# A routing, a mixture of experts and an MLP on one core: low parts of the last weights taken a step later in the first routing, and more idle products

## The chip, the cores and the metric

The kernel runs on one core of a Trainium2 chip. The metric is the device time in microseconds (us) of one execution: the median of three runs is 817.9 us (817.57 to 819.57). Engines are named as in the profile: PE (TensorE, with its weight loads PEld), DVE (VectorE), ACT (ScalarE), POOL (GpSimd) and SP (SyncE, which here only issues transfers).

## The reference, cut to what matters

```python
# 1 attention with a state per head: (4, 8, 768, 40) -> rows x of 3072 tokens, 320 wide
# 2 experts: every token goes to one of 8 experts, 384 tokens each
logits = x @ w_gate
order = np.argsort(-logits.flatten())
for idx in order:                       # best (token, expert) pairs first
    tok, e = int(idx) // E, int(idx) % E
    if assigned[tok] >= 0 or counts[e] >= cap: continue
    assigned[tok] = e; counts[e] += 1
for e in range(E):
    mask = assigned == e
    out[mask] = np.maximum(x[mask] @ w1[e], 0.0) @ w2[e]
# 3 a common MLP on all tokens
h = out @ w_in                          # 320 -> 2048
g = np.where(h > 0, h, np.exp(np.minimum(h, 0)) - 1)
return g @ w_out                        # 2048 -> 320
```

Here `w_in` and `w_out` come as 64-bit floats. The kernel fetches their words and puts 32-bit floats together from them on the chip.

## The kernel before, in words

Attention runs first, until about 167 us, 24 units of work in a fixed order. The routing then finds, in eight rounds, one expert each, which expert fills up next and which 384 tokens it takes. Round 0 has nothing else to hide behind: the products of expert 0 need its tokens. So round 0 is written out by hand in `Mlp.start` (L1340), and the seven later rounds are woven into the products.

A round is a search: in each of six steps DVE compares 24 values per partition with 32 candidates (`ge`, L713), PE counts (L727), DVE folds the counts (L590 to L596), PE sums them (L748), and DVE picks the digit (L751, L754). Step 0 uses a comparison that was made during attention (L737). At the end DVE marks the tokens (L773 to L777), writes which weights to fetch (`wi`, L765), PE numbers the tokens (L783 to L785), and after twelve more products (L810) DVE writes the list of tokens, `idx` (L816).

Between these steps `start` calls a generator, `fill` = `wout_pieces` (L942), ten times. It prepares the last weights, `w_out`, in 16 chunks of 128 x 320. Chunk i goes through these pieces: SP fetches its words (L856, two chunks ahead); ACT takes the absolute value and, in one of two variants, the sign (L868, L870) and DVE shifts (L873); DVE puts the bits together (L880) and POOL multiplies by the sign (L883); ACT or DVE copies the rounded high part to `woh` (L972 or L974); POOL subtracts it to leave the low part `wol` (L965). In the other variant DVE adds the sign (L877) instead of ACT and POOL. Each `yield` ends a piece and says which engine the next one needs. One call of `start` runs pieces until a piece whose need names DVE ("d") is followed by a piece whose need names DVE too:

```python
while True:
    d = "d" in need
    _, need = next(fill)
    if d and "d" in need:
        break
```

What is left of the 16 chunks when round 0 ends is done among the products of expert 0, piece by piece, by a planner (`Mlp.run`). The planner counts expected engine times, runs a piece of `wout` first of all side work where its time has come, and holds it back where DVE's expected backlog is over 2 us. It pauses side work from the last product of the first MLP layer (`C0` = 7) until the first output product. The output product of chunk f (`C2`, L1234, L1235, L1238) needs both `woh` and `wol` of chunk f.

When `idx` is known, POOL issues three gathers of token rows (`xg`, L984 by `get_x`) behind three gathers of expert weights (`stg`). PE transposes each row tile when it has landed (L1049), ACT and DVE split it into two parts (L1066, L1057), and then the products of expert 0 start (L1096). Between these, PE runs idle products (`spin`, L1035) whose results nobody reads: `WARM` = [8, 2, 2, 2] says how many stand ahead of each transposed tile and behind the last. Engines run their own queue in order, so an idle product delays what stands behind it.

Of the kernel before, what the change touches and what calls it, by code (L numbers as in the profile page):

```python
# [8 lines left out]
F32 = mybir.dt.float32  # L9
# [4 lines left out]
ALU = mybir.AluOpType  # L14
# [14 lines left out]
FU = 3  # L29
SPIN, MX = 12, [256, 512, 640]  # L30
NB, NL, PX = 2, 3, 0.2
WARM = [8, 2, 2, 2]


class Plan:
# [46 lines left out]
    def next(self):  # L82
        self.due(min(self.todo)[0])
# [741 lines left out]
class Mlp:  # L825
# [115 lines left out]
    def wout_pieces(self):  # L941

        nc = self.nc
        wide = self.wout.dtype != F32
        n = 320
        tiles = {}

        def get(i):
            x = self.pool.tile([128, n, 2], I32, name="wx", bufs=3) if wide else None
            t = self.pool.tile([128, 2, n], F32, name="wt", bufs=2)  # L950
            tiles[i] = (x, t[:, 1], t[:, 0])
            self.fetch([(slice(0, 128), self.src(self.wout, slice(0, 128), slice(i * n, i * n + n)))], wide, tiles[i])

        get(0)
        get(1)
        yield
        for i in range(16):
            if i < 14:
                get(i + 2)
            F = tiles[i][2]  # L960
            yield self.plan.t, "d"
            yield from self.conv(wide, tiles.pop(i), not self.router.res or self.plan.pick(p=821 + PD, d=402) == "p")
            t = self.copy(self.woh[:, i], F, 360, 240)
            yield t, "p"
            nc.gpsimd.tensor_tensor(self.wol[:, i], F, self.woh[:, i], op=ALU.subtract)  # L965
            self.plan.on("p", 821)
            self.wdone = i + 1

    def copy(self, out, x, a, d):

# [69 lines left out]
    def prep_x(self, r):  # L1040
# [6 lines left out]
        def turn(k):  # L1047
            for t in range(3):
                nc.tensor.transpose(ps[k][0][:, t * 128:t * 128 + 128], self.xg[k][:, t * 128:t * 128 + 128], self.ident)  # L1049

        def split(k):
            p, slot = ps[k]
            p = p.rearrange("p (t n) -> p t n", t=3)
            h, l = (x[:, :, k * 128:k * 128 + 128] for x in (xh, xl))

            def rest():
                nc.vector.tensor_tensor(l, p, h, op=ALU.subtract)  # L1057
                slot[0] = plan.on("d", 469)
                if k == 2:
                    self.xst[r] = (xh, xl)  # L1060
                    self.xready[r] = slot[0]

            if r:
                plan.later(self.copy(h, p, 371, 469), rest)
            else:
                nc.scalar.activation(h, p, AF.Copy)  # L1066
                plan.on("a", 371)
                rest()

        if r == 0:  # L1070
            ps = [self.psum() for t in range(3)]
            for k in range(3):
                self.spin(WARM[k])
                turn(k)
                split(k)
            self.spin(WARM[3])
            return
# [262 lines left out]
    def start(self, first):  # L1340

        nc = self.nc
        fill = self.fill
        self.ws = {}
        early = []
        need = "d"
        for k, (_, _, gap) in enumerate(first):
            if gap and k > FK:
# [3 lines that stand above are left out]
                    if d and "d" in need:  # L1352
                        break
            if not early and 0 in self.router.res:
                for i in range(3):
                    self.get_w(0, i)
                early = [q for i in range(3) for q in self.pieces(i)]
        self.routed = 0
        self.get_x(0)
        for h, l, x, p in early:  # L1360
            nc.scalar.activation(h, x, AF.Copy)
        for k, (h, l, x, p) in enumerate(early):
            nc.vector.tensor_tensor(l[p], x[p], h[p], op=ALU.subtract)
            if k % 2 and k < 4:
                self.get_w(0, 3 + k // 2)
        self.wsplit = 3
        routes = self.routes(1)
        for _ in range(R1):
            next(routes)
        plan = self.plan  # L1370
        plan.reset()
        self.junk = self.acc.tile([128, 512], F32, name="acc")
        for _ in self.prep_x(0):
            pass
        return fill, routes
# [134 lines left out]
```

## Time and profile before

| | value |
|---|---|
| median of three runs | 817.9 us |
| profiled execution, its own time | 817.59 us |
| its span, first to last instruction | 815.8 us |
| mean granted clock of PE | 0.925 of 2.4 GHz |
| busy: PE, DVE, ACT, POOL | 89%, 72%, 43%, 38% |

The profile gives for each instruction its start and its length, and for idle time before it what ended that idle time. "Granted clock" is the share of 2.4 GHz that PE was given; it has two levels, 0.5 (1.2 GHz) and 1.0 (2.4 GHz), and a value between them is a mean over a stretch in which it changed. A line such as L972 can be that of a helper that several callers use.

### The profile page before, as it was taken

How to read it: one execution, taken by the hardware profiler on the slowest of the kernel's cores; microseconds unless marked ns; L12 is line 12 of the kernel's file. 1: busy time of each engine (PE TensorE's matmuls, PEld its weight loads, DVE VectorE, ACT ScalarE, POOL GpSimd, SP SyncE). 2: the span in 40 equal slices, each digit the busy share in tenths (PEclk: the TensorE clock that was granted, in tenths of full speed). 3: DMA queues.
4: the chain of work that ended last, by engine and by line, in shares of the span. 5: the costliest groups of instructions: out<-in, count | busy, mean ns of one | idle time of the engine just before them, and what ended most of it. 6: DMA issues, size and time to landing. Idle time of an engine off the chain costs nothing.

```text
span 815.8 us, 18330 instructions
## 1 busy us (share of the span) xinstructions
PE 729.8 (89%) x7355; PEld 681.9 (84%) x7355; DVE 586.1 (72%) x1616; ACT 348.5 (43%) x743; POOL 309.2 (38%) x358
## 2 busy tenths in 40 slices
PE   7788788836899799799999999999999999999995
PEld 5678678725788789789989988898999999999995
DVE  8697878777979976987897679867733942862542
ACT  5343334324356533543553255325533633742431
POOL 3687887626425631633134125213410601201001
PEclk8678787856999999999999999999999999999998
DMA  8766855135114202112123103200500410100000
GB/s 343 253 216 209 278 186 187 43 107 199 54 30 139 83 27 78 51 44 100 32 65 93 40 0 106 67 27 0 172 12 13 138 35 25 65 1 26 1 1 25
DMA packets 20757, 72.79 MB, mean 89 GB/s; under 512 B 3200, under 2 KB 7296, under 8 KB 19264
## 3 DMA queue, kind: packets, MB, share of 16 engines
q1 hardware_dynamic: 8336, 35.08, 12.6%
q0 software_dynamic: 8448, 31.73, 11.8%
q10 hardware_dynamic: 3888, 4.82, 2.1%
q8 instruction: 58, 0.95, 0.5%
q14 instruction: 27, 0.22, 0.1%
HBM read 62.96 MB, written 8.65 MB: 88 GB/s over the span
## 4 chain that ended last, share of the span: by engine, by line
PE 58%; DVE 21%; issue 8%; ACT 4%; DMA 4%; POOL 2%; ACTq 1%; SPq 0%; POOLq 0%; DVEq 0%
PE ph L1096 24%; PE acc L1234 5%; PE acc L1238 4%; PE acc L1235 4%; PE acc L1203 3%; PE acc L1205 3%; PE acc L1204 3%; DVE e L1149 2%; DMA xd<-x 2%; PE pr L727 2%; DVE ge L713 1%; DVE gl L980 1%; PE acc L1190 1%; PE pX L448 1%; DMA vk<-in_vk_dram 1%
## 5 line engine op out<-in xcount | busy, mean ns | idle before, releaser
L1234 PE MATMUL acc<-woh,gh 128*128 128x320 f32 x384 | 122.7, 320 | 0.0
L1238 PE MATMUL acc<-woh,gl 128*128 128x320 f32 x384 | 119.7, 312 | 0.0
L1235 PE MATMUL acc<-wol,gh 128*128 128x320 f32 x384 | 119.0, 310 | 0.0
L1149 DVE SCALAR_TENSOR_TENSOR e<-e,ph 128x384 f32<-128x384 f32 x128 | 69.9, 549 | 61.8 <-ACT e L1146 61.4
L1145 ACT ACTIVATE e<-ph 128x384 f32<-128x384 f32 x128 | 62.7, 489 | 116.3 <-PE ph L1096 112.0
L980 POOL TENSOR_TENSOR gl<-e,gh 128x384 fp32r<-128x384 f32 x33 | 34.8, 1057 | 164.3 <-DVE gh L974 132.3
L1096 PE MATMUL ph<-yh,wih 128*128 128x384 f32 x256 | 89.7, 351 | 0.4
L1096 PE MATMUL ph<-yh,wil 128*128 128x384 f32 x256 | 86.2, 337 | 0.0
L1113 ACT ACTIVATE gh<-ph 128x384 fp32r<-128x384 f32 x64 | 31.3, 491 | 121.9 <-PE ph L1096 120.7
L1244 POOL DMA_INDIRECT out_dram<-ot,idx x24 | 24.0, 1001 | 141.3 <-ACT ot L972 138.1
L1120 DVE SCALAR_TENSOR_TENSOR gl<-ph,gh 128x384 fp32r<-128x384 f32 x64 | 35.4, 556 | 56.8 <-ACT gh L1113 56.4
L1238 PEld LDWEIGHTS acc<-woh,gl 128*128 128x128 f32 x384 | 72.5, 189 | 0.6
L1234 PEld LDWEIGHTS acc<-woh,gh 128*128 128x128 f32 x384 | 72.8, 190 | 0.2
L1235 PEld LDWEIGHTS acc<-wol,gh 128*128 128x128 f32 x384 | 72.7, 189 | 0.0
L1146 ACT ACTIVATE e<-e 128x384 f32<-128x384 f32 x128 | 67.3, 526 | 4.0
L1096 PE MATMUL ph<-yl,wih 128*128 128x384 f32 x256 | 66.5, 341 | 0.0
L980 DVE TENSOR_TENSOR gl<-e,gh 128x384 fp32r<-128x384 f32 x95 | 57.3, 607 | 1.9
L1096 PEld LDWEIGHTS ph<-yh,wih 128*128 128x128 f32 x256 | 48.4, 189 | 4.5 <-ACT yh L1208 4.4
L1096 PEld LDWEIGHTS ph<-yh,wil 128*128 128x128 f32 x256 | 48.3, 189 | 0.0
L1096 PEld LDWEIGHTS ph<-yl,wih 128*128 128x128 f32 x256 | 46.4, 189 | 0.0
L1096 PE MATMUL ph<-xh,w1h 128*128 128x384 f32 x128 | 45.0, 352 | 0.2
L1203 PE MATMUL acc<-gh,w 128*128 128x384 f32 x128 | 44.6, 349 | 0.0
(269 smaller groups left out, 2023.5 us busy)
## 6 DMA issues: line engine op xcount, KB each, us to landing
vk<-in_vk_dram SPq DMA_DIRECT2D x12, 968.0 KB, 8.7
qk<-in_qk_dram SPq DMA_DIRECT2D x11, 1024.0 KB, 8.0
wx<-in_wout_dram SPq DMA_DIRECT2D x16, 320.0 KB, 2.8
xd<-x ACTq DMA_DIRECT2D x48, 96.0 KB, 3.7
cx<-in_win_dram SPq DMA_DIRECT2D x8, 512.0 KB, 4.4
qk<-in_qk_dram SPq DMA_DIRECT2D x2, 512.0 KB, 5.9
cx<-in_win_dram SPq DMA_DIRECT2D x4, 256.0 KB, 4.2
xg<-xd,idx POOLq DMA_INDIRECT x24, 3.3
```

The source lines that it names most:

```text
L980: (self.nc.vector if e == "d" else self.nc.gpsimd).tensor_tensor(out, x, y, op=ALU.subtract)
L1096: PE.matmul(p, w, x, start=k == 0, stop=k == 7)
L1113: nc.scalar.activation(h, p, AF.Relu)
L1120: nc.vector.scalar_tensor_tensor(l, p, 0.0, h, op0=ALU.max, op1=ALU.subtract)
L1145: nc.scalar.activation(e, p, AF.Relu, scale=-1.0)
L1146: nc.scalar.activation(e, e, AF.Exp, scale=-1.0)
L1149: nc.vector.scalar_tensor_tensor(e, e, -1.0, p, op0=ALU.add, op1=ALU.max)
L1203: PE.matmul(p, w[:, c], h, start=f == 0, stop=False)
L1204: PE.matmul(p, w[:, cl], h, start=False, stop=False)
L1234: PE.matmul(p, h[:, c], self.woh[:, f], start=f == 0, stop=False)
L1235: PE.matmul(p, h[:, c], self.wol[:, f], start=False, stop=False)
L1238: PE.matmul(p, l[:, c], self.woh[:, f], start=False, stop=f == 15)
```

## The change: a piece of the fill moves, and idle products are added

Four things change. First, in round 0 the low part of a chunk is no longer subtracted right behind its copy; it is kept in `late` and issued in front of the next chunk's copy (`self.routed < 0` holds only in round 0). The copy then no longer ends with `yield t, "p"`. Second, the tile `wt` (two halves, two buffers) becomes two tiles: `wa` with the pool's two buffers and `wt` with three. Third, `WARM` grows from [8, 2, 2, 2] to [20, 3, 3, 3]. Fourth, six idle products are issued as soon as `wi` of round 0 is written, and the accumulator they write is taken earlier for that. The buffers of the output rows, `ot`, stay three.

```diff
-WARM = [8, 2, 2, 2]
+WARM = [20, 3, 3, 3]
...
-            t = self.pool.tile([128, 2, n], F32, name="wt", bufs=2)
-            tiles[i] = (x, t[:, 1], t[:, 0])
+            tiles[i] = (x, self.pool.tile([128, n], F32, name="wa"), self.pool.tile([128, n], F32, name="wt", bufs=3))
...
+        def low(i, F):
+            nc.gpsimd.tensor_tensor(self.wol[:, i], F, self.woh[:, i], op=ALU.subtract)
+            self.plan.on("p", 821)
+            self.wdone = i + 1
+
+        late = None
...
             yield from self.conv(wide, tiles.pop(i), not self.router.res or self.plan.pick(p=821 + PD, d=402) == "p")
+            if late:
+                late = low(*late)
             t = self.copy(self.woh[:, i], F, 360, 240)
+            if self.routed < 0:
+                late = i, F
+                continue
             yield t, "p"
-            nc.gpsimd.tensor_tensor(self.wol[:, i], F, self.woh[:, i], op=ALU.subtract)
-            self.plan.on("p", 821)
-            self.wdone = i + 1
+            low(i, F)
...
+        self.junk = self.acc.tile([128, 512], F32, name="acc")
         self.ws = {}
...
             if not early and 0 in self.router.res:
+                self.spin(6)
                 for i in range(3):
...
         plan.reset()
-        self.junk = self.acc.tile([128, 512], F32, name="acc")
         for _ in self.prep_x(0):
```

## Rows read from the trace of the kernel before

**Rows 1.** Busy time by stretch: start and end, length, then busy us (and instructions) of PE, PEld, DVE, ACT and POOL, then PE's granted clock, the transfers' share and GB/s. The stretches are the search of round 0, the arrival of the tokens, and five stretches of the products.

```profile
166.00:186.50 20.50, 4.89 (x63) 3.80 (x63) 17.70 (x80) 6.52 (x15) 6.98 (x8) 0.50 0.36 106
192.00:200.00 8.00, 6.15 (x21) 4.11 (x19) 5.30 (x11) 4.29 (x9) 5.26 (x5) 0.56 0.69 235
200.00:216.00 16.00, 12.72 (x74) 11.80 (x75) 15.06 (x41) 7.51 (x17) 8.39 (x9) 1.00 0.28 92
216.00:238.00 22.00, 21.14 (x126) 18.66 (x125) 15.88 (x58) 9.25 (x19) 4.15 (x5) 0.92 0.15 45
238.00:278.00 40.00, 32.85 (x217) 30.70 (x216) 38.62 (x104) 23.50 (x50) 23.78 (x24) 0.99 0.28 88
278.00:295.00 17.00, 16.93 (x106) 15.56 (x107) 16.27 (x52) 10.13 (x23) 8.70 (x10) 0.91 0.24 79
295.00:816.00 521.00, 499.27 (x3152) 474.95 (x3151) 339.94 (x978) 220.56 (x449) 132.18 (x144) 0.99 0.15 49
```

**Rows 2.** The timeline of DVE in the search: start, length, line, operation. The comparisons of steps 1, 3 and 5 (of five; step 2's is as long as step 1's, step 4's as step 5's), and two of the instructions that mark the tokens.

```profile
169.43 0.56 DVE L713 TENSOR_TENSOR ge<-d,kx 128x768 bf16<-128x768 bf16 x1
...
175.31 1.11 DVE L713 TENSOR_TENSOR ge<-d,kx 128x768 bf16<-128x768 bf16 x1
...
182.05 1.10 DVE L713 TENSOR_TENSOR ge<-d,kx 128x768 bf16<-128x768 bf16 x1
185.48 0.65 DVE L773 SCALAR_TENSOR_TENSOR AB<-d,j,a 128x24 f32<-128x24 f32 x1
186.05 0.23 DVE L774 SCALAR_TENSOR_TENSOR AB<-d,j,a 128x24 f32<-128x24 f32 x1
```

**Rows 3.** The timeline of POOL in the same stretch, with idle time before an instruction and its releaser in brackets, and the first gather of token rows.

```profile
175.12 0.88 POOL L965 TENSOR_TENSOR wol<-wt,woh 128x320 fp32r<-128x320 f32 x1 [0.58 <-ACT woh L972]
177.05 0.87 POOL L883 TENSOR_TENSOR wt<-wt,wx 128x320 f32<-128x320 f32 x1 [1.04 <-issue]
...
185.22 0.87 POOL L965 TENSOR_TENSOR wol<-wt,woh 128x320 fp32r<-128x320 f32 x1 [0.58 <-ACT woh L972]
192.18 0.95 POOL L984 DMA_INDIRECT xg<-xd,idx  x1 [1.42 <-DVE inc L820]
194.73 1.21 POOL L984 DMA_INDIRECT xg<-xd,idx  x1 [0.30 <-issue]
```

**Rows 4.** The timeline of DVE in steps 2 and 3: pieces of the fill and the search's instructions behind them.

```profile
174.49 0.31 DVE L873 TENSOR_SCALAR wt<-wx 128x320 int32<-128x320 int32 x1
176.43 0.48 DVE L880 SCALAR_TENSOR_TENSOR wt<-wt 128x320 int32<-128x320 int32 x1
176.98 0.17 DVE L590 SCALAR_TENSOR_TENSOR fold<-pr,rem 32x8 f32<-32x8 f32 x1
178.21 0.17 DVE L751 TENSOR_REDUCE j<-pr 128x1 f32<-128x8 f32 x1
```

**Rows 5.** The timeline of PE from the numbering of the tokens to the first product of expert 0. A row with x8 is eight instructions, from the first start to the last end.

```profile
186.62 0.20 PE L783 MATMUL pr<-mm,ones 128*128 128x48 bf16 x1 [1.72 <-DVE mm L777]
189.44 0.99 PE L810 MATMUL pr<-R,ge 128*128 128x48 bf16 x12 [2.55 <-DVE R L803]
190.24 3.76 PE L1038 MATMUL acc<-wih 128*128 128x512 f32 x8
195.74 0.90 PE L1049 MATMUL ph<-ident,xg 128*128 128x128 f32 x3 [1.74 <-DMA xg<-xd,idx]
196.29 1.20 PE L1038 MATMUL acc<-wih 128*128 128x512 f32 x2
198.79 0.61 PE L1049 MATMUL ph<-ident,xg 128*128 128x128 f32 x3
...
199.98 0.44 PE L1096 MATMUL ph<-xh,w1h 128*128 128x384 f32 x1
```

**Rows 6.** The chain of work that ended last, around the first gather: start, length, what.

```profile
192.18 3.52 DMA xg<-xd,idx
...
199.43 0.50 ACT xh L1066
```

**Rows 7.** Busy time by stretch again (columns as in rows 1), two stretches of 2 us: before and at the rise of the clock.

```profile
192.00:194.00 2.00, 2.00 (x5) 0.99 (x3) 1.57 (x4) 0.75 (x3) 1.52 (x2) 0.50 0.83 318
198.00:200.00 2.00, 1.89 (x9) 1.15 (x8) 0.60 (x2) 0.98 (x2) 0.66 (x1) 0.74 0.83 264
```

**Rows 8.** What PE and its weight loads waited for from 200 to 300 us: us in total, times, the longest.

```profile
PEld ph L1049 <- DVE e L1149: 5.0, 1, 5.0
...
PE pr L727 <- DVE ge L713: 4.0, 2, 3.2
```

**Rows 9.** The timeline of POOL and PE among the products of expert 0: the low parts of chunks 9, 14 and 15, and the first output product of chunk 15.

```profile
244.90 0.88 POOL L965 TENSOR_TENSOR wol<-wt,woh 128x320 fp32r<-128x320 f32 x1 [2.70 <-DVE woh L974]
276.88 0.86 POOL L965 TENSOR_TENSOR wol<-wt,woh 128x320 fp32r<-128x320 f32 x1
286.52 0.87 POOL L965 TENSOR_TENSOR wol<-wt,woh 128x320 fp32r<-128x320 f32 x1
293.70 0.30 PE L1234 MATMUL acc<-woh,gh 128*128 128x320 f32 x1
```

**Rows 10.** DVE and POOL in one timeline at 205 us: three POOL subtractions back to back, and a DVE instruction of 8 values per partition that starts beside the first of them.

```profile
205.51 3.45 POOL L980 TENSOR_TENSOR w<-stg,w 128x512 fp32r<-128x512 f32 x3
205.70 1.26 DVE L690 SCALAR_TENSOR_TENSOR rem<-neg,rem 128x8 f32<-128x8 f32 x1
```

## Prediction

> **What bounds the kernel now.** I read the busy time by stretch first [rows 1]. From 295 us PE is busy 499 of 521 us at a granted clock of 0.99: the change touches nothing there. The change acts where PE isn't the bound. In the search of round 0 DVE is busy 17.7 of 20.5 us and PE 4.9; then the tokens' arrival takes until 200 us. After that come two stretches in which DVE is nearly full (15.1 of 16 us, and 38.6 of 40 us) while PE loses 3.3 and 7.2 us. So the end moves with the first product of expert 0, at 199.98 [rows 5], and with what DVE-bound work stands behind it.
>
> The timeline of DVE comes second [rows 2]. The same comparison takes 0.56 us in steps 1 and 2 and 1.10 in steps 3 to 5. POOL's timeline [rows 3] shows why: a low part L965 begins 0.19 us before each long one and runs 0.88 us. The comparison of 175.31 ends at 176.42, 0.42 after POOL's end at 176.00, so it waits for POOL's whole instruction and then runs in about 0.45. In the same way L773 takes 0.65 beside the L965 of 185.22, where its neighbour L774 takes 0.23.
>
> Third is the chain of waits: `idx`, then 3.52 us for a gather, transposes, 0.50 on ACT, first product [rows 6]. PE's timeline there [rows 5] shows idle products at 1.2 GHz: eight in 3.76 us, and before the tail of the last one that is 512 columns / 1.2 GHz = 0.427 each.
>
> **The change part by part.** *The order of the fill.* A call stops where two needs in a row name DVE. Before, copy and low part went with the next chunk's shift in one call, two calls a chunk. Without the yield for POOL the copy is a call of its own: three calls a chunk. Ten calls then finish: fetch; chunk 0 shift, L880 with L883, copy; chunk 1 the same with the low part of 0 before its copy; chunk 2 the same with the low part of 1. Chunk 2's low part stays pending. Before it was four whole chunks and the fifth's shift.
>
> Step by step, in times of before:
> - Step 3: no POOL beside the comparison of 175.31, 1.11 to 0.56: -0.55. Behind its fold now stands L880 (0.48) where L873 (0.31) stood [rows 4]; the digit waits for DVE, +0.13.
> - Step 4: L883 follows L880's start by 0.62 (176.43 to 177.05 [rows 3, 4]), so it now runs from about 177.9 to 178.8 and meets the comparison, which starts at about 178.25. It waits for L883's end and runs 0.45: 1.0 instead of 1.10, -0.1. The pending low part of chunk 0 follows on POOL.
> - Step 5: POOL has ended by 180.1, the comparison starts at about 181.5: -0.55. Its fold meets chunk 2's L883 at the end, +0.1.
> - Marking: chunk 1's low part ends at about 184.5, when L773 begins: 0.65 to 0.23, -0.4.
>
> Sum: -0.55 + 0.13 - 0.1 - 0.55 + 0.1 - 0.4 = -1.4 us on `wi` and `idx`. Bounds: -0.5 if step 4 and the marking still collide, -1.9 if nothing does. The gathers stand behind the low part of chunk 1 on POOL, which has ended by then; SP only fetches one chunk less. The third `wt` buffer has no wait that I find: chunk i+3 writes it after the low part of chunk i in order of issue.
>
> *The rule that speaks against it.* Among the products a DVE instruction that starts beside the first of three POOL subtractions back to back takes 1.26 us, one POOL instruction (3.45 / 3 = 1.15) and not three [rows 10]. The Trainium skill (SBUF — State Buffer, Who interferes with whom) says that the first to start takes the shared ports for its whole instruction and the other blocks fully. It doesn't say who is next where POOL has a second instruction ready; if POOL kept the ports, step 4's comparison would also wait for the pending low part, and the gain would be 0.9 less. The row is against that, and I keep -1.4.
>
> *Six idle products behind `wi`.* The numbering products run at 186.62, the twelve products L810 at 189.44 [rows 5], 2.8 us later. Six idle ones take 6 x 0.427 = 2.56 us: they fit with 0.1 to 0.2 to spare; I take 0, at worst +0.3.
>
> *Twenty, three, three, three.* L810 would end at 190.43 - 1.4 = 189.0, and the first token tile would land at 195.74 - 1.4 = 194.3. In between 5.3 us: twenty idle products take 8.5 us at 1.2 GHz and 4.3 at 2.4. Before, 3.8 us of idle products from 190.24 followed by a gap left the clock at 0.50, and it rose at about 199.0 (the mean 0.74 of 198 to 200 [rows 7]) after nearly unbroken work from 195.74. Now PE works without a gap from 185.3 on. If the clock rises between 189 and 193, the twenty end between 193.3 and 195.1: on time, or 0.8 late. The first two tiles have slack of that size, since the third gather, issued 2.55 us after the first [rows 3], sets the end: cost 0 to 0.4, I take 0.1.
>
> What that buys: the third tile landed by 198.3 (194.73 + 3.5, [rows 3, 6]), its transposes waited for two idle products at 1.2 GHz until 198.79 and ended at 199.4. At 2.4 GHz they start on landing and last about 0.45 (between half of the 0.90 at 195.74 and the 0.61 of 198.79, in which the clock rose): -0.65. The three idle products behind (3 x 0.213 = 0.64) lie beside ACT's 0.50: 0 to +0.1.
>
> First product: -1.4 + 0.1 - 0.65 = -2.0, at about 198.0. Both kernels then run it at 2.4 GHz.
>
> *What is late next.* The fill now leaves 13 chunks and a low part for the products, against 11 chunks and three of four pieces: 52 pieces against 47, a lag of 1.25 chunks. In DVE's time that is at least L873 + L880 + L873 = 1.1 us, up to 2.7 with L877 and copies. The planner holds a piece back when DVE's backlog is over 2 us, so in the full stretches the lag isn't made up; it comes out at the end. Chunk 15's low part ends at 287.39, its product starts at 293.70 [rows 9]: slack 6.3. From chunk 9 to chunk 15 the rate is (286.52 - 244.90) / 6 = 6.9 us a chunk, or 6.1 without the 5.0 us in which PE stood still [rows 8]. Lag 1.25 x 6.1 = 7.6, less 6.3: PE waits 1.3 us for chunk 15. Bounds: 0 (the planner forces the pieces before PE is there, the gl and weight pieces give way) and 2.3 at 6.9, beyond which lies a rival. A wait of PE lets DVE catch up, so some of it comes back where PE waits for DVE later; I take +1.1.
>
> Sum: 817.59 - 2.0 + 1.1 = 816.7 for the profiled execution; the median of the runs shown is 0.3 above it.
>
> **The rivals.**
> - *Faster, the lag is covered.* The wait at chunk 15 doesn't come, and one of the drops of PE's clock goes. Two are in [rows 1]: 216 to 238 at 0.92 (22 x 0.08 = 1.76 us lost) behind a wait of 3.2 us for `ge` [rows 8], and 278 to 295 at 0.91 (1.5 us) behind the 5.0 us wait. For it: both hang on waits that a different order of the pieces shifts. Against: DVE has more to do. 817.6 - 2.0 - 1.7 = 813.9.
> - *Slower, the low part of the last chunk.* Its place is PE's wait ahead of chunk 15's first product; price at the last chunk's own pace, 286.52 - 276.88 = 9.6 us: 1.25 x 9.6 - 6.3 = 5.7, so 817.6 - 2.0 + 5.7 = 821.3. It decides from a lag of 8.3 us on (slack 6.3 + gain 2.0). For it: the pace falls towards the end. Against: the 9.6 hold the 5.0 us wait of PE.
> - *The clock doesn't rise in time.* All twenty run at 1.2 GHz: they end at 189.0 + 8.5 = 197.5, 3.2 us behind the first tile; three instead of two between the tiles add 0.85. From first transposes to first product it was 4.2 us, so the first product comes at 197.5 + 4.2 + 0.85 = 202.6, 2.6 later than before: 821.3 with the 1.1. Against: 3.3 us of steady work raised it at 199.
> - *No change of substance.* The comparisons still collide, in step 4 for two POOL instructions (the rule above) or by a shift of some tenths: gain 1.1 or less at the first product, 817.6.
>
> **How the numbers follow.** Forecast 0.42 (816.7, its own range 815.2 to 818.6), covered lag 0.27 (813.9), late low part 0.18, cold idle products 0.05, no substance 0.08. A measurement here tells about 0.3% from no change, 2.5 us: faster means below 815.4, slower above 820.4. Faster: nearly all of the second case and a tenth of the first, 0.31. Slower: three quarters of the late low part, and the cold products, with a little of the forecast: 0.20. Same: 0.49. The range leaves out the edges of the second and third cases: 813.0 to 821.0.
>
> **What would show it.** Right: comparisons of 0.56, 0.56, 0.56, about 1.0, 0.56 and L773 at 0.23; the first gather at about 190.8; a granted clock of 1.0 before the first transposes; L1096 at about 198.0; chunk 15's L965 ending after its place in PE's queue, with a wait of PE on it. Wrong: a long comparison in step 3 or 5; transposes that wait for idle products and not for the gather; `fold` or L810 behind the six; a first product later than 199; or a sum that is decided after 300 us, by waits for `ge` of later rounds that moved, which nothing here prices.

## The result and the profile after

The changed kernel takes 826.6 us (median of six runs, 824.65 to 828.47) where before takes 817.74 on the same chip: a ratio of 1.0102, with a 95% interval of 1.0068 to 1.0136. It is slower by some 1%, outside the predicted range of 813.0 to 821.0. The profiled execution took 826.66 us, with a span of 824.9. Ratios here leave out executions that ran slow as a whole, and of the profiles only that of f1 below is of such a one (840.5 us), with its extra time ahead of round 0: step 1's comparison starts there at 179.59 us instead of 169.46.

The lines of the changed kernel behind L965 are 8 higher than before's (L1096 is now L1104); the low part L965 is now L954, so that L980 is here the copy on ACT and L988 the subtraction that was L980. I place the time with three marks that both traces have: the comparison of step 1, the first product of expert 0, and the first transfer of output rows (`ot`, POOL) of an expert.

| stretch (one profile each) | before | after | difference |
|---|---|---|---|
| step 1's `ge` to the first gather | 22.75 us | 21.99 us | -0.8 |
| first gather to the first product | 7.80 us | 6.97 us | -0.8 |
| first product to the first output transfer of expert 0 | 95.07 us | 104.52 us | +9.45 |
| from there to the first output transfer of the next expert | 86.10 us | 87.40 us | +1.3 |
| from there to the end of the span | 434.65 us | 434.56 us | -0.1 |

Up to the first product the change does most of what was forecast; the loss lies among the products of expert 0. Here are the changed kernel's busy times in the stretches of [rows 1], with the arrival of the tokens in two parts (columns as there):

```profile
190.00:192.00 2.00, 2.00 (x7) 1.54 (x6) 1.79 (x10) 1.15 (x2) 0.55 (x1) 0.59 0.89 307
192.00:200.00 8.00, 8.00 (x42) 6.29 (x41) 5.72 (x11) 4.67 (x9) 4.48 (x5) 1.00 0.69 218
200.00:216.00 16.00, 12.11 (x65) 11.51 (x64) 15.65 (x39) 7.40 (x17) 8.52 (x8) 0.89 0.24 80
...
238.00:278.00 40.00, 33.47 (x211) 31.50 (x210) 37.56 (x97) 24.01 (x52) 21.04 (x21) 0.94 0.31 96
278.00:295.00 17.00, 14.45 (x80) 12.98 (x81) 16.44 (x43) 9.31 (x21) 11.97 (x12) 0.83 0.23 79
```

The clock is at 1.00 from 192 on, where it was 0.56 before. But from 200 to 216, from 238 to 278 and from 278 to 295 it is lower than in [rows 1] (0.89, 0.94 and 0.83 against 1.00, 0.99 and 0.91), and in the last of these PE is busy 14.45 us of 17 where it was 16.93. Only from 216 to 238 is it higher (1.00 against 0.92).

The search follows. First DVE in step 4 and at the marking, then POOL (both in the manner of [rows 2, 3]):

```profile
177.89 0.92 DVE L754 TENSOR_SCALAR d<-h,j 128x24 bf16<-128x24 f32 x1
178.84 1.17 DVE L713 TENSOR_TENSOR ge<-d,kx 128x768 bf16<-128x768 bf16 x1
...
182.25 0.56 DVE L713 TENSOR_TENSOR ge<-d,kx 128x768 bf16<-128x768 bf16 x1
...
185.12 0.23 DVE L773 SCALAR_TENSOR_TENSOR AB<-d,j,a 128x24 f32<-128x24 f32 x1
```

```profile
177.91 0.87 POOL L883 TENSOR_TENSOR wt<-wt,wx 128x320 f32<-128x320 f32 x1 [3.34 <-issue]
178.74 0.86 POOL L954 TENSOR_TENSOR wol<-wt,woh 128x320 fp32r<-128x320 f32 x1
...
191.45 0.94 POOL L992 DMA_INDIRECT xg<-xd,idx  x1 [1.46 <-DVE inc L820]
```

The comparisons of steps 1 to 3 and 5 take 0.56 us and L773 0.23, as forecast. Step 4 does not. L754, just ahead of the comparison, already meets POOL's L883 (0.92 us where it took 0.24 before) and ends at 178.81, 0.03 behind it. By then the low part L954 has run on POOL since 178.74. The comparison, which starts at 178.84, ends 0.41 after it: it waits for a second POOL instruction.

PE from the numbering of the tokens to the first product, as in [rows 5]:

```profile
185.95 2.91 PE L1046 MATMUL acc<-wih 128*128 128x512 f32 x6
188.67 1.03 PE L810 MATMUL pr<-R,ge 128*128 128x48 bf16 x12
189.50 5.81 PE L1046 MATMUL acc<-wih 128*128 128x512 f32 x20
195.25 0.55 PE L1057 MATMUL ph<-ident,xg 128*128 128x128 f32 x3
...
198.42 0.45 PE L1104 MATMUL ph<-xh,w1h 128*128 128x384 f32 x1
```

The clock rises inside the twenty idle products (0.59 in the mean from 190 to 192, 1.00 after), so the first transposes run at 2.4 GHz and take 0.55 us instead of 0.90.

Now the stretch that loses. This view is what PE waited for there (198.42 to 302.94) in the changed kernel: the waiting instruction, its releaser, us in total, times, the longest.

```profile
PE pr L727 <- DVE ge L713: 4.5, 5, 1.7
PE acc L1196 <- DVE w L988: 3.9, 1, 3.9
PE ph L1104 <- DVE e L1157: 3.6, 1, 3.6
PE pr L810 <- DVE R L803: 1.7, 1, 1.7
PE pr L748 <- DVE fl L596: 1.3, 2, 1.1
PE acc L1242 <- ACT woh L980: 1.0, 1, 1.0
PE acc L1243 <- POOL spc L1251: 0.5, 1, 0.5
PE acc L1246 <- POOL gl L988: 0.3, 1, 0.3
```

Before, the same view (199.98 to 295.05) has the wait for `e` of [rows 8] and few others:

```profile
PE ph L1049 <- DVE e L1149: 4.7, 1, 4.7
PE pr L727 <- DVE ge L713: 4.0, 2, 3.2
PE pr L670 <- DVE X L667: 1.5, 1, 1.5
PE pr L748 <- DVE fl L596: 0.7, 1, 0.7
PE pr L810 <- DVE R L803: 0.3, 1, 0.3
```

The whole stretch, before and after (columns as in [rows 1]):

```profile
199.98:295.05 95.07, 83.70 (x519) 76.78 (x520) 85.89 (x252) 50.44 (x107) 45.03 (x47) 0.96 0.24 77
198.42:302.94 104.52, 87.39 (x520) 79.41 (x520) 94.30 (x254) 52.64 (x114) 48.38 (x48) 0.93 0.24 75
```

The sums of the waits are 11.2 and 16.8 us: +5.6. Apart from its waits, PE is busy with the same products, 83.70 us before and 87.39 after: +3.7, as more of them run at 1.2 GHz. The granted clock is 0.50 from 209 to 212, behind the wait for `w`, and its mean over the stretch falls from 0.96 to 0.93. Together these are 9.3 of the 9.45 us. The wait that the prediction priced, for chunk 15, is there (L1242 and L1243, from 299.7 on), and it is 1.5 us; the 0.3 of L1246 stands ahead of chunk 0. The larger ones it did not have: 3.9 us for `w` at 208.28, and 1.7 for `R`.

The wait for `w` in the timelines of DVE and POOL, as in [rows 10]:

```profile
202.23 1.22 DVE L676 TENSOR_SCALAR neg<-rem 128x8 f32<-128x8 f32 x1
203.37 1.45 DVE L988 TENSOR_TENSOR w<-stg,w 128x512 fp32r<-128x512 f32 x1
...
207.82 0.41 DVE L988 TENSOR_TENSOR w<-stg,w 128x256 fp32r<-128x256 f32 x1
```

```profile
201.28 0.89 POOL L883 TENSOR_TENSOR wt<-wt,wx 128x320 f32<-128x320 f32 x1 [3.57 <-ACT w L980]
202.13 1.30 POOL L988 TENSOR_TENSOR w<-stg,w 128x512 fp32r<-128x512 f32 x1
203.38 2.16 POOL L954 TENSOR_TENSOR wol<-wt,woh 128x320 fp32r<-128x320 f32 x2
205.50 1.38 POOL L988 TENSOR_TENSOR w<-stg,w 128x512 fp32r<-128x512 f32 x1
```

POOL runs the two late low parts (chunks 2 and 3) back to back between its `w` subtractions, and the planner gives more of `w` to DVE: before, POOL took three of them in a row from 205.51 [rows 10]; here DVE takes one at 203.37 (1.45 us, beside the low parts) and the last at 207.82. PE's product follows that one at 208.28. PE's own products stand in another order, too.

The low parts of chunks 13, 14 and 15, in POOL's timeline as in [rows 9]:

```profile
286.24 0.88 POOL L954 TENSOR_TENSOR wol<-wt,woh 128x320 fp32r<-128x320 f32 x1 [0.78 <-ACT woh L980]
292.88 1.41 POOL L954 TENSOR_TENSOR wol<-wt,woh 128x320 fp32r<-128x320 f32 x1
300.71 0.86 POOL L954 TENSOR_TENSOR wol<-wt,woh 128x320 fp32r<-128x320 f32 x1 [3.87 <-ACT woh L980]
```

Chunk 15 is 14.2 us later than before, almost twice the 7.6 that the prediction took. But PE comes there late itself: chunk 15's first product starts at 300.68, after a wait of 1.0, where it started at 293.70 before.

### The profile page after: what moved, and what is told of

Its sections match the earlier page's. It is cut to its first block, busy times and chain, and to the rows that moved or that the text cites. A ratio compares the mean times of both kernels' runs of the same rounds, so it can differ in the third digit from the quotient of the medians.

```text
span 824.9 us, 18360 instructions
## 1 busy us (share of the span) xinstructions
PE 735.4 (89%) x7376; PEld 686.1 (83%) x7376; DVE 592.2 (72%) x1615; ACT 348.5 (42%) x745; POOL 310.0 (38%) x356
## 3 DMA queue, kind: packets, MB, share of 16 engines
q0 software_dynamic: 8448, 31.73, 11.6%
## 4 chain that ended last, share of the span: by engine, by line
PE 60%; DVE 21%; issue 9%; ACT 5%; POOL 3%; DMA 1%; ACTq 1%; POOLq 0%; DVEq 0%
PE ph L1104 24%; PE acc L1242 5%; PE acc L1243 4%; PE acc L1246 4%; PE acc L1211 3%; PE acc L1213 3%; PE acc L1212 3%; PE pO L368 2%; DVE e L1157 2%; PE pX L448 2%; DVE gl L988 2%; PE pO L382 2%; PE pr L727 2%; DVE ge L713 2%; PE acc L1198 1%
## 5 line engine op out<-in xcount | busy, mean ns | idle before, releaser
L1242 PE MATMUL acc<-woh,gh 128*128 128x320 f32 x384 | 123.7, 322 | 1.0 <-ACT woh L980 1.0
L1246 PE MATMUL acc<-woh,gl 128*128 128x320 f32 x384 | 120.8, 315 | 0.3 <-POOL gl L988 0.3
L1243 PE MATMUL acc<-wol,gh 128*128 128x320 f32 x384 | 120.1, 313 | 0.5 <-POOL spc L1251 0.5
L988 POOL TENSOR_TENSOR gl<-e,gh 128x384 fp32r<-128x384 f32 x34 | 35.4, 1043 | 170.5 <-DVE gh L982 142.7
L1104 PE MATMUL ph<-yh,wih 128*128 128x384 f32 x256 | 90.8, 355 | 4.0 <-DVE e L1157 3.6
L1104 PE MATMUL ph<-yh,wil 128*128 128x384 f32 x256 | 87.1, 340 | 0.0
L1242 PEld LDWEIGHTS acc<-woh,gh 128*128 128x128 f32 x384 | 73.5, 191 | 1.6 <-ACT woh L980 1.3
L1246 PEld LDWEIGHTS acc<-woh,gl 128*128 128x128 f32 x384 | 73.4, 191 | 1.2 <-POOL gl L988 0.6
L1243 PEld LDWEIGHTS acc<-wol,gh 128*128 128x128 f32 x384 | 73.4, 191 | 0.8 <-POOL spc L1251 0.8
L1104 PE MATMUL ph<-yl,wih 128*128 128x384 f32 x256 | 66.3, 340 | 0.0
L988 DVE TENSOR_TENSOR gl<-e,gh 128x384 fp32r<-128x384 f32 x94 | 58.1, 622 | 1.9
L1104 PEld LDWEIGHTS ph<-yh,wih 128*128 128x128 f32 x256 | 49.3, 192 | 8.5 <-ACT yh L1216 4.6
L1104 PEld LDWEIGHTS ph<-yh,wil 128*128 128x128 f32 x256 | 49.0, 192 | 0.0
L1104 PEld LDWEIGHTS ph<-yl,wih 128*128 128x128 f32 x256 | 46.5, 189 | 0.0
L1104 PE MATMUL ph<-xh,w1h 128*128 128x384 f32 x128 | 44.5, 348 | 0.0
```

What stands on the lines that cost most here:

```text
L988: (self.nc.vector if e == "d" else self.nc.gpsimd).tensor_tensor(out, x, y, op=ALU.subtract)
L1104: PE.matmul(p, w, x, start=k == 0, stop=k == 7)
L1242: PE.matmul(p, h[:, c], self.woh[:, f], start=f == 0, stop=False)
L1243: PE.matmul(p, h[:, c], self.wol[:, f], start=False, stop=False)
L1246: PE.matmul(p, l[:, c], self.woh[:, f], start=False, stop=f == 15)
```

## The experiments

Medians of before differ from chip to chip (817.7 to 823.6 us), so each run is told by its ratio to before on the same chip. "Products" is the stretch from the first product of expert 0 to the first output transfer in the one profile of a run (before 95.07, after 104.52), "PE waits" the sum of PE's waits in it (11.2 and 16.8). Where a time stands in place of the ratio, there is one execution of each kernel.

| run | ratio, interval | products | PE waits |
|---|---|---|---|
| e1_idle_only | 1.0008, 0.9977 to 1.0039 | 96.33 | 11.8 |
| e2_fill_only | 1.0121, 1.0060 to 1.0181 | 103.52 | 18.0 |
| e3_late_two_calls | 1.0028, 0.9997 to 1.0060 | 101.07 | 15.5 |
| e4_seven_calls | 1.0083, 1.0060 to 1.0106 | 104.56 | 17.0 |
| e5_eight_calls | 828.36 us, before 825.89 | 97.17 | 11.2 |
| e6_fourteen_calls | 825.33 us, before 825.89 | 94.36 | 10.6 |
| e12_twelve_calls_idle | 1.0059, 1.0029 to 1.0088 | 97.27 | 12.6 |
| e8_after_short_pool | 1.0053, 1.0021 to 1.0085 | 95.05 | 11.6 |
| e8_before_short_pool | 0.9993, 0.9953 to 1.0033 | 89.33 | 8.8 |
| e7_before_slack1500 | 825.72 us, before 825.89 | 98.67 | 13.2 |
| e13_before_slack1500 (e7's kernel, timed) | 1.0047, 1.0020 to 1.0074 | 98.73 | 13.8 |
| e11_after_slack1500 | 829.38 us, before 825.89 | 101.18 | 13.1 |
| f2_after_slack1500 (e11's kernel, timed) | 1.0050, 1.0013 to 1.0087 | 100.37 | 13.7 |
| f3_before_slack1000 | 1.0042, 1.0012 to 1.0071 | 101.41 | 14.5 |
| f4_after_slack1000 | 1.0127, 1.0063 to 1.0190 | 105.59 | 19.1 |
| f1_after_order_less_work | 1.0107, 1.0074 to 1.0140 | 104.52 | 16.8 |
| f5_burst | 1.0007, 0.9984 to 1.0029 | 96.36 | 11.4 |
| f6_after_again | 1.0097, 1.0060 to 1.0135 | 103.78 | 15.9 |

**The change in its two parts.** e1 adds only the idle products to before; e2 takes them away from after and leaves only the change of the fill.

```diff
-WARM = [8, 2, 2, 2]
+WARM = [20, 3, 3, 3]
...
+                self.spin(6)
```

> Of the change only the idle products (six behind the weights' indices, and 20, 3, 3, 3 around the transposes); the fill of the search as before. Theory A (the search's shorter fill leaves two more chunks of the last weights, with their POOL work, to the products of expert 0, and DVE then waits for POOL there): the first product of expert 0 about 0.6 us earlier, no change behind it, 817.0 (816.0 to 818.2). Theory B (the idle products cost the time, through the clock or the transposes): 820 or more. Theory C (any other order of the planner's pieces costs): the order of pieces is that of before, so as A.

```diff
-WARM = [20, 3, 3, 3]
+WARM = [8, 2, 2, 2]
...
-                self.spin(6)
```

> Of the change only the fill (the low part a step later, three calls a chunk, three wt buffers); idle products 8, 2, 2, 2 as before. Theory A: as the changed kernel less the 0.6 us that its idle products gain, 826.5 to 828. Theory B: 816 to 818. Theory C: as A.

The idle products cost nothing and gain little: from step 1's comparison to the first product e1 needs 29.66 us against 30.55, and its products stand as before's, in the same order on every engine. The fill alone carries the whole loss (1.0121), and the two ratios (+0.08% and +1.21%) show no sign that the parts act on each other: both together are +1.02%.

**The yield.** e3 keeps the low part a step later but ends the copy with the yield again, so that a chunk takes two calls as before.

```diff
             if self.routed < 0:
                 late = i, F
+                yield t, "p"
                 continue
```

> The changed kernel, but with the yield for POOL kept behind the copy in the search, so that a chunk takes two calls as before: four chunks are copied in the search and only one low part stays pending. Theory A: the lag is one low part, so the products run as before and the start is 1 to 1.5 us earlier: 816.5 (815 to 818). Theory C (the loss is not the lag but that the planner's order, drawn for one state of the fill, becomes another): anything from 817 to 828, with no relation to the lag; 820 or more speaks for it.

All five comparisons take 0.56 us here, step 1 to the first gather takes 21.39 us (1.36 less than before), and the first product comes 2.0 earlier. Only one low part is left over. Still the products last 101.07 us, with a wait for `w` of 3.8 us like after's. The next stretch gives some of it back (83.2 us against 86.1), and the time is before's or a little more (1.0028, with 1 inside the interval). So one low part left over already costs 6.0 us in this stretch, though the whole time does not show a loss clearly.

**How many calls.** e4, e5, e6 and e12 leave the low part where before had it and run 7, 8, 14 and 12 calls in round 0 instead of 10; e12 has the idle products too.

```diff
+        calls = 0
...
-            if gap and k > FK:
+            calls += bool(gap and k > FK)
+            if gap and k > FK and calls <= 7:
```

> The kernel before with seven calls of the fill in the search instead of ten: two and a half chunks done, the low parts where they were, idle products as before. The search is then free of POOL in its last steps, about 1 us shorter. Theory A: the lag is 1.75 chunks, about that of the changed kernel, so 824 to 828. Theory C: anything from 817 to 828. Theory D (the moved low part itself costs, by its place or its third buffer, not the number of chunks): 816.5 to 818.

> The kernel before with eight calls of the fill in the search instead of ten: one chunk less is ready when the products start. Read is the stretch from the first product of expert 0 to its first output transfer: 95.1 us before, 104.5 changed. Theory A (chunks left over for the products cost there): between the two, 98 to 102. Theory C (the order that the planner draws costs, whatever is left over): anything from 93 to 105.

```diff
+            calls += bool(gap and k > FK)
+            for _ in range((1 + (calls in (2, 4, 6, 8))) * bool(gap and k > FK)):
```

> The kernel before with fourteen calls in the search (two calls in four of its ten gaps): two chunks more are ready. The search gets longer, by 1 to 3 us. Theory A: the stretch falls below 95, to 87 to 92. Theory C: anything from 93 to 105, and no less likely above 95 than below.

> The kernel before with the changed kernel's idle products and twelve calls of the fill in the search: one chunk more is ready instead of two fewer. Theory A: the search 2 to 3 us longer, the idle products give back 0.9, the products of expert 0 are 2 to 3 shorter: 0.3 to 2 us faster than before, ratio 0.997 to 1.001. Theory C: ratio anywhere from 0.995 to 1.010.

A lag of a chunk and a half (six pieces, as many as the change leaves over), made by fewer calls, costs the products 9.5 us (e4). That is after's loss, but by other waits: 12.1 of e4's 17.0 us are for `ge` and none for `w`. A lag of one chunk costs 2.1 (e5). Two chunks more in the search save 0.7 in the products and cost 5.1 ahead of them (e6: 35.68 us from step 1 to the first product), and twelve calls are no better. The loss doesn't grow evenly with the lag, as a plain debt of work would: 6.0 us for one low part (e3), 2.1 for four pieces, 9.5 for six.

**The POOL instructions.** e8 leaves the order as it is in both kernels and shortens the fill's multiplication and subtraction on POOL, among the products, to 8 of 320 columns. The other columns of sign and low part are left out; the low parts are cleared ahead of the search.

```diff
...
+            c = slice(0, n if self.routed < 0 else 8)
+            nc.gpsimd.tensor_tensor(F[:, c], F[:, c], hi.bitcast(F32)[:, c], op=ALU.mult)
...
-            nc.gpsimd.tensor_tensor(self.wol[:, i], F, self.woh[:, i], op=ALU.subtract)
+            c = slice(0, 320 if self.routed < 0 else 8)
+            nc.gpsimd.tensor_tensor(self.wol[:, i, c], F[:, c], self.woh[:, i, c], op=ALU.subtract)
```

> The changed kernel, the order of all engines as it is, but among the products POOL's two instructions for a chunk of the last weights (the sign and the low part) work on 8 columns instead of 320: signs and low parts of the other columns are left out, and one clear of the low parts stands ahead of the search. Theory P (DVE loses the time because POOL holds what it needs while both run): the DVE time over the shortest of each form in the stretch to the first output transfer falls from 32 to 20 or less, and the stretch from 104.5 to 92 to 97. Theory W (it is the fill's work on DVE itself that is late): the stretch falls by less than 3.

> The same cut in the kernel before. Theory P: the DVE time over the shortest falls from 23 to about 16, the stretch from 95 to 88 to 91, and the distance between the two kernels' stretches from 9.5 to 5 or less. Theory W: falls by less than 3, and the distance stays.

The stretch of the products, for after and for before so shortened (columns as in [rows 1]):

```profile
204.69:299.74 95.05, 83.17 (x520) 75.40 (x520) 83.33 (x254) 52.61 (x114) 34.83 (x48) 0.98 0.27 84
```

```profile
198.35:287.68 89.33, 80.48 (x519) 74.00 (x520) 79.87 (x252) 50.41 (x107) 33.15 (x46) 1.00 0.25 81
```

DVE's 254 instructions take 83.33 us here and 94.30 in after. So DVE's time in this stretch is in good part time beside POOL: 9.5 us of after's products and 5.7 of before's go with it. But 5.7 us between the two orders remain, and 0.6% in the timed pair (1.0053 and 0.9993, with intervals that overlap a little). POOL's part of the difference is some 3.7 of 9.4 us by these profiles, one of each kernel, where the same order repeats within 1.3 us.

**Other orders.** The planner's hold-back of 2 us for `wout` is set to 1.5 and 1.0, with the fill as before and as after. This draws other orders of the side work, with and without the lag.

```diff
-SLACK = dict(rows=600, routes=3000, weights=1000, wout=2000)
+SLACK = dict(rows=600, routes=3000, weights=1000, wout=1500)
```

> The kernel before with the planner's allowance for the last weights at 1.5 us of backlog instead of 2: the search and what is left over as before, the pieces among the products in another order. Theory A: the stretch stays at 94 to 97. Theory C: it moves by more than 3 us.

> The changed kernel with the same allowance of 1.5 us: the search and the lag as changed, the pieces in another order. Theory A: the stretch stays at 102 to 107. Theory C: it moves by more than 3 us, and may fall to 95.

> The kernel before with the planner's allowance at 1.5 us, timed: another order of the pieces with nothing more left over. Theory A: ratio 0.998 to 1.003. Theory C: 1.005 or more.

> The changed kernel with the planner's allowance at 1.5 us, timed; the kernel before with it was 1.0047 of before. Theory A: 1.008 to 1.015, that plus the lag. Theory C: 1.000 to 1.006, another draw of the order with the same lag.

> The kernel before with the allowance at 1.0 us: a third draw of the order with the search as before. Theory A: 0.998 to 1.004. Theory C: 1.003 to 1.010.

> The changed kernel with the allowance at 1.0 us, the pair of the run before it. Theory A: slower than its pair by 0.005 to 0.012. Theory C: the pair differs by less than 0.005, with either sign.

Without any lag at the start, other orders already cost 0.47% and 0.42%: before's order is a good draw. The lower allowances also hold the fill back longer (chunk 15's low part starts 86.5 us behind the first product in before, 89.4 in e13 and 99.0 in f3), so these runs don't part an order from the lateness of pieces that belongs to it. The lag adds 0.03% at 1.5 us and 0.85% at 1.0, each uncertain by 0.5% or more, against 1.02% at 2.0. It has no fixed price; what it does depends on the order that comes out. In f4 the wait that the prediction priced is the largest: 9.3 of PE's 19.1 us are for the high and low parts of chunks 12 to 15.

**The order without the work.** f1 has after's order of instructions, but what the lag adds is cut: the low part of chunk 2 and all pieces of chunk 3 work on 8 columns of 320, and their other columns are left out. Of the six pieces left over, only the shift of chunk 4 (0.31 us of DVE) stays whole.

```diff
...
+            c = slice(0, 8 if i in (2, 3) else 320)
+            nc.gpsimd.tensor_tensor(self.wol[:, i, c], F[:, c], self.woh[:, i, c], op=ALU.subtract)
...
+            if i == 3:
+                x, F = (x[0][:, :8], x[1][:, :8], x[2][:, :8]), F[:, :8]
...
+            t = self.copy(self.woh[:, i, :8] if i == 3 else self.woh[:, i], F, 360, 240)
```

> The changed kernel with the order of all its queues as it is, but the work that it left over for the products cut: the low part of chunk 2 and all of chunk 3 work on 8 columns instead of 320 (left out are their other columns; a clear of three chunks' tiles stands ahead of the search). Theory A (the work left over costs): the stretch to the first output transfer falls from 104.5 to 95 to 99, ratio to before 0.998 to 1.003. Theory C (the order that the planner draws for the lagging fill costs, whatever the instructions do): stretch 101 to 105, ratio 1.006 to 1.011.

The loss stays whole: 1.0107. The five longest of PE's waits among the products:

```profile
PE pr L727 <- DVE ge L713: 6.6, 7, 1.8
PE ph L1110 <- DVE e L1163: 3.9, 1, 3.9
PE pr L810 <- DVE R L803: 1.9, 1, 1.9
PE pr L748 <- DVE fl L596: 1.3, 2, 1.0
PE acc L1202 <- DVE w L994: 1.3, 1, 1.3
```

The wait for `w`, beside the shortened low parts, is 1.3 us, where after, e2 and f6 show 2.0 to 3.9. The waits for `ge` are 6.6, where those show 4.5 to 6.8, and the sum of all is 16.8 again.

**The work without the order.** f5 keeps the changed round 0 and all idle products. What then lacks against before (the two pending low parts, chunk 3, the first piece of chunk 4) is issued in one go while the tokens arrive, and the planner's clocks are put back, so that every engine's order among the products is exactly before's. The part of the edit that is left out here, in `wout_pieces`, copies chunk 3 on ACT, issues both pending low parts behind it, and gives chunks 3 and 4 the variants that they have in before. f6 is the changed kernel again, on the same chip.

```diff
...
         self.get_x(0)
+        for k in range(4):
+            next(fill)
...
+        next(fill)
         plan.reset()
         for _ in self.prep_x(0):
             pass
+        at = dict(plan.at)
+        next(fill)
+        plan.at = at
```

> Round 0 as in the changed kernel (three calls a chunk, low parts a step later, all idle products), but what then lacks against before (chunk 3, the two pending low parts, the first piece of chunk 4) is issued in one go while the tokens arrive, between idx and the first product, so that the planner starts from before's state and every engine's order among the products is exactly before's. Theory A (the loss lies in the order that the planner draws for the lagging fill): the products cost what they cost before, 95 to 97 us from the first product to the first output transfer, and the gain at the first product is kept less the price of the burst, 0.5 to 1.5 us: ratio 0.997 to 1.002. Theory B (later low parts, or the idle products, hurt in themselves): the loss stays, 102 us or more, ratio 1.007 to 1.012.

> The changed kernel once more, beside the burst on the same chip. Theory A: 1.008 to 1.013 and about 104 us from the first product to the first output transfer, at least 0.6% above the burst. Theory B: no more than 0.3% from the burst.

The medians are 819.56 us for f5, 827.78 for f6 and 818.79 for before. PE's waits among the products, first of f5, then of f6 (f5's lines L1064, L1111, L1135 and L1164 are before's L1049, L1096, L1120 and L1149):

```profile
PE ph L1064 <- DVE e L1164: 4.6, 1, 4.6
PE pr L727 <- DVE ge L713: 4.0, 2, 3.1
PE pr L670 <- DVE X L667: 1.4, 1, 1.4
PE pr L748 <- DVE fl L596: 0.7, 1, 0.7
PE ph L1111 <- DVE gl L1135: 0.4, 1, 0.4
PE pr L810 <- DVE R L803: 0.3, 1, 0.3
```

```profile
PE pr L727 <- DVE ge L713: 4.5, 5, 1.7
PE ph L1104 <- DVE e L1157: 3.4, 1, 3.4
PE acc L1196 <- DVE w L988: 2.7, 1, 2.7
```

(Of f6 the three longest.) f5's waits are before's almost to the tenth, in 96.36 us of products; f6's are after's within 1.2 us each, in 103.78. With before's order given back, 8.2 us of median go. f5 reaches its first product 29.77 us after step 1's comparison, 0.8 less than before and 0.8 more than after (the price of the burst), and that is too small a gain to be told from no change. By the traces DVE and ACT run the same instructions in the same order among the products in after, e2, e8's after, f1 and f6, and likewise in before, e1 and f5 (there with chunk 4's first piece just behind the first product). No version here with all its work beat before clear of noise.

## Why the prediction was wrong, by its steps

The step that failed is "what is late next". It took the lag for a debt of 1.25 chunks that comes out at one place, PE's wait for chunk 15, at +1.1 us. That wait is 1.5 us. The stretch costs 9.45 more, by the mechanism that the step passed over: the fill is planned piece by piece among the products, so a fill that stands further back makes the planner draw another order for all of them. In that order PE waits at other places (+5.6 us), and its clock falls behind some of the waits (+3.7). f1 and f5 show it from both sides: the order without the work keeps the loss, and the changed round 0 that starts the products from before's state, in before's order, has none. The prediction had seen that another order shifts waits, but priced it only as a gain, in the rival "faster"; as a loss it stands only among the signs of being wrong, placed after 300 us, with the words "which nothing here prices".

The step also has a slip in its count: 13 chunks of four pieces and a low part are 53 pieces, not 52, so the lag is 1.5 chunks. By its own rate that makes a wait of 1.5 x 6.1 - 6.3 = 2.9 us for chunk 15, further from the measured 1.5, and a sum of some 818.5, still 8 us short.

Two assertions in that step fell with it. "The planner holds a piece back" at a backlog of 2 us was taken to pace the fill; in after, the low parts came 8.3 us later than before at chunk 9 and 14.2 at chunk 15, and 1.5 us in place of 2 drew an order that cost less (f2). And "a wait of PE lets DVE catch up" was the reason to take +1.1 out of 0 to 2.3; the fill caught up nothing.

The rival "slower, the low part of the last chunk" came nearer (821.3), but for a reason that isn't so: it too has the loss in PE's wait at chunk 15, and there it isn't. Its price of 5.7 is almost four times the wait measured there; that its sum is nearer is luck.

The search gained 0.8 instead of 1.4 us. Step 3, step 5 and the marking came as forecast. Step 4 is the term that was mis-sized: the prediction had the comparison wait for L883 alone (1.0 us, 0.1 less than before). It lost instead: L754 was held 0.68 us by L883, and the comparison then waited for the pending low part too. The Trainium skill (SBUF — State Buffer, Who interferes with whom) has the other engine blocked fully while one has the shared ports. The trace agrees: L754 took 0.92 us and the comparison 1.17. (L754 starts 0.02 us ahead of L883 in the profile and waits all the same; starts so close don't show who was first.) The case that the prediction set aside from [rows 10], that POOL's second instruction goes ahead of a DVE instruction that already waits, is not what happened: the one that waited at L883's end was L754, and the comparison was 0.10 late for its turn. The term that was left out is L754. e3 has no such collision and gains 1.36, near the sum predicted, but with the fill in another order.

The clock came as forecast: it rose inside the twenty idle products, which ended by the time the first tile's transposes began. From the first gather to the first product 0.8 us went where +0.1 - 0.65 was forecast. The six idle products cost nothing that shows, in after and in e1.

The other 1.3 us, between the first output transfers of the two experts, belong to before's profile more than to the change: e1 (87.22) and f5 (87.27), with before's order, need as long there as after (87.40).

What stays open is which of the moved pieces costs how much. In the four profiles of after's order (after, e2, f1, f6) the wait for `w` is 1.3 to 3.9 us and that for `ge` 4.5 to 6.8, while the sum stays between 15.9 and 18.0: what one place saves another takes, so the 5.6 us of waits can't be shared out piece by piece; e8 only says that some 3.7 us of the difference go with POOL's time.

## What to carry to other kernels

Where a planner or a list places side work, a small change to what is left over is a new order for everything behind it: price it by the spread of other orders (here 95 to 106 us for one stretch, with the kernel before near the good end), not by the work that moved. To take a local gain without that risk, hand the planner the state that it had before; whether the gain then shows is a question of its size. And before you explain a loss by work that was added, cut that work and keep the order: here the loss stayed.

## What was not expected of the hardware

A DVE instruction that waits for POOL can cost the one behind it its turn too. In step 4 L754 ended at 178.81, 0.03 us behind POOL's L883. By then POOL's next instruction, the low part, had run since 178.74, and the comparison that started at 178.84 waited for all of it and ended at 180.01. In [rows 10] the DVE instruction of 205.70 ended at 206.96, just behind the first of POOL's three, which ended at 206.92; behind it an L873 that started at 207.42, beside the second one, took 0.95 us where [rows 4] shows 0.31. A small size does not spare the wait: L754, with 24 values per partition, took 0.92 us beside POOL and 0.24 without.

The granted clock stayed at 0.50 through the search and rose at about 191.7 us in the changed kernel, after PE had worked without a gap since its numbering products at 185.85. In before, with eight idle products and a gap behind them, it rose at 199.
